# Ranks of single score tiles and weight chunks, and inverse sums loaded in two halves, in a fused attention and two-MLP kernel

## The chip, the cores and the metric

The kernel runs on one core of one Trainium2 chip. The metric is the device time in microseconds (us) of one execution; less is better. The engines are named as in the profile: PE (TensorE), PEld (its weight loads), DVE (VectorE), ACT (ScalarE), POOL (GpSimd) and SP (SyncE, which issues nearly all DMAs).

## The reference

Three layers follow each other, all in float32.

```python
scores = scale * q @ k.T                      # 4 batches, 8 heads, 576 x 576, head size 64
scores = where(scores >= max(scores) - tau, scores, -1e6 * 1000)
attn = exp(scores - max(scores))
attn = attn / (sum(attn) + 1e-9)
x = (attn @ v)                                # to 2304 tokens x 512
h = x @ w_in                                  # 512 x 2048
y = (h * sigmoid(h)) @ w_out                  # 2048 x 512
out = ((y @ w_a) * (y @ w_b)) @ w_o2          # 512 x 1536, 1536 x 512
```

## The kernel before, in words

**Stages.** Attention works on pairs of heads (16 pairs over 4 batches); each pair has a block of 4 score tiles (queries 0 to 255) and one of 5 tiles (queries 256 to 575), 144 tiles of 128 x 576 in all. In the first batch all the blocks of 4 come first, then the blocks of 5. A tile goes through these steps in `softmax` (L506): `scores` on PE into a PSUM bank (L530, from tile 54 on L523); `lowest` on DVE, which scales and finds the minimum (L539); `threshold` on DVE (L547, L545 in the first 16 tiles); `exp` on ACT (L553, L551 in the first 16); `mask` on DVE, which zeroes what lies under the threshold and sums the rest (L556). The first 16 tiles take turns in two banks, `sa` and `sb`; from then on `sa` alone is used and is free again after `lowest`. `weigh` (L575) transposes the masked tile on PE (`turn`, L589), copies it out on ACT (L597, L599), and multiplies by v (`values`, L638).

**The sums.** The masked weights are not divided; the product is. DVE inverts the sums (L488), PE transposes them beside the product (L643), ACT copies both to SBUF (`evacuate`, L659). A small DMA stores the inverse sums to DRAM (`store_sums`, L663), a second one loads them back, spread over 64 partitions for each of the two heads (`load_sums`, L670), POOL multiplies (`divide`, L673) and a third DMA stores x, transposed, to DRAM (`store`, L677). There is one buffer for x and one for the loaded sums. From tile 54 on, each head's q and k (one buffer, `qk0`) are split into two parts by ACT (L448), DVE (L451) and POOL (L454) ahead of the scores.

**The first MLP** reads x back by blocks of 256 tokens (later 512) (`load_x`, L727) and runs unit by unit: `mlp1_up` (L766), tanh and gate (L776 to L785), `mlp1_down` (L826). It fills PE beside attention and goes on alone once attention has ended. Its weights come in 32 chunks of 512 KB; `split_weight` (L326) loads one (L345) and takes it apart: ACT (L349, L354), DVE (L360, `join` L365), a sum on POOL or DVE (L370), the high part on ACT (L374), the low part on DVE (L378). A unit needs its chunks.

**The second MLP** (L1133, L1219) streams prepared weights and has no part in the change.

**The order** is worked out in Python while the kernel is built, by the class `Plan`. Each step is a task with an engine, a cost, a rank and the tasks it waits for. `run` plays the tasks through by their costs; an engine that comes free takes the ready task of the lowest rank:

```python
                if kind == "ready":
                    heapq.heappush(ready[x["engine"]], (x["rank"], x["n"]))
```

The order so found is then written out, and on the chip every engine runs its list strictly in that order. Score tile n has rank n (its mask n - 1, its transposes n + `R_T`, its q/k load n + `R_LD`); first-MLP units have ranks from `R_MLP` = 1000 up and so give way to attention; weight chunk i has rank `W_AT + W_STEP * i`, 2 + 1.3 i. DMAs are tasks of SP with a landing time of their cost, size and a `slack`. Where the plan shows idle time of PE ahead of a transpose, `turn` puts dummy transposes in front of it (L586), one for each 109 ns of 60% of that gap, at most 16.

## Time and profile before

| | us |
|---|---|
| median of 3 runs (lowest, highest) | 1130.11 (1128.37, 1130.49) |
| the profiled execution, its own time | 1129.17 |
| span of the profile | 1127.4 |
| PE busy (share of the span) | 1097.6 (97%) |
| DVE busy | 830.4 (74%) |
| ACT busy | 571.5 (51%) |
| POOL busy | 163.9 (15%) |

The span runs from the first to the last instruction of the program; the time of an execution holds a little around it. Busy shares are means over stages with different limits: attention with the first MLP beside it lasts until about 505 us, the rest of the first MLP until about 729 us, the second MLP to the end. The granted clock of PE was 0.996 of full speed over the span. Which engine paces a stage is read from the windows and waits of that stage.

### The profile page before, as it was taken

Reading aid. Unit: us, or ns where it says so; the run is one execution under the profiler, and the core shown is the slowest. Engines: PE = TensorE matmul, PEld = TensorE weight load, DVE = VectorE, ACT = ScalarE, POOL = GpSimd, SP = SyncE. Lnnn points to the kernel's source line nnn. Section 1 sums busy time; section 2 is a strip of 40 time slices with the busy share of each in tenths; the row PEclk is TensorE's granted clock in tenths of the full one; section 3 lists DMA queues with packets and bytes.
Section 4 is the critical chain, followed back from the end, with each engine's and each line's share of the span. In section 5 each row is a group of like instructions: output and inputs, shape, how many; then the busy total and the mean of one; then the engine's idle time right before and its main releaser. Section 6 shows DMA issues by size and latency. Waiting matters only on the chain.

```text
span 1127.4 us, 19460 instructions
## 1 busy us (share of the span) xinstructions
PE 1097.6 (97%) x7104; PEld 980.1 (87%) x7104; DVE 830.4 (74%) x1722; ACT 571.5 (51%) x1012; POOL 163.9 (15%) x308
## 2 busy tenths in 40 slices
PE   8879989999999999999999999999999999999998
PEld 6557767988899888899988888899999999999998
DVE  7878988888888898866898884256884668536664
ACT  6877776777677776765666552211242114401132
POOL 2452101323433433213000000000000000000000
PEclk9999999999999999999999999999999999999999
DMA  5564552544544343326898844488889888888882
GB/s 181 188 191 136 178 176 76 162 123 131 164 133 138 128 152 124 91 69 203 281 312 275 275 154 162 152 253 257 250 309 304 256 254 253 277 285 251 251 253 80
DMA packets 114975, 222.27 MB, mean 197 GB/s; under 512 B 8112, under 2 KB 75328, under 8 KB 114880
## 3 DMA queue, kind: packets, MB, share of 16 engines
q1 hardware_dynamic: 114736, 221.03, 61.9%
q8 instruction: 56, 0.92, 0.3%
q14 instruction: 39, 0.32, 0.1%
q10 hardware_dynamic: 144, 0.00, 0.0%
HBM read 173.74 MB, written 47.26 MB: 196 GB/s over the span
## 4 chain that ended last, share of the span: by engine, by line
PE 58%; DMA 1%; issue 1%; POOL 0%; DVE 0%; ACT 0%; SPq 0%; DVEq 0%; ACTq 0%
PE pr L1133 23%; PE pr L1219 11%; PE hb L766 6%; PE hc L766 5%; PE sb L826 3%; PE yc L826 2%; PE yd L826 2%; PE ye L826 2%; PE yf L826 2%; PE av L638 1%; PE tp L589 1%; DMA yr<-yT_d 1%; PE sa L523 1%; DMA qk<-qk 0%; POOL sp L454 0%
## 5 line engine op out<-in xcount | busy, mean ns | idle before, releaser
L1133 PE MATMUL pr<-w 128*128 128x384 f32 x1512 | 262.6, 334 | 0.0
L1133 PEld LDWEIGHTS pr<-w 128*128 128x128 f32 x1512 | 262.2, 188 | 0.1
L766 PE MATMUL hb<-xh,w 128*128 128x256 f32 (+1 forms) x704 | 157.5, 314 | 5.6 <-DVE th L779 4.6
L766 PEld LDWEIGHTS hb<-xh,w 128*128 128x128 f32 x704 | 114.3, 192 | 17.5 <-DVE th L779 5.8
L1219 PE MATMUL pr<-zh,w 128*128 128x384 f32 x504 | 128.4, 336 | 0.0
L556 DVE SCALAR_TENSOR_TENSOR e<-t,thr,e 128x576 f32<-128x576 f32 x128 | 109.7, 857 | 18.0 <-ACT e L553 16.6
L539 DVE TENSOR_SCALAR_CACHE_REDUCE t<-sa,nscale 128x576 f32<-128x576 f32 x128 | 103.8, 811 | 20.0 <-PE sa L523 16.3
L589 PE MATMUL tp<-ident,e 128*128 128x128 f32 (+1 forms) x706 | 106.1, 279 | 9.5 <-DVE e L556 6.6
L553 ACT ACTIVATE e<-t,min 128x576 f32<-128x576 f32 x128 | 99.3, 776 | 27.5 <-DVE t L539 27.2
L766 PE MATMUL hb<-xl,w 128*128 128x256 f32 (+1 forms) x352 | 107.7, 306 | 0.0
L589 PEld LDWEIGHTS tp<-ident,e 128*128 128x128 f32 (+1 forms) x706 | 76.6, 135 | 32.2 <-issue 15.1
L826 PE MATMUL sb<-gh,w 128*128 128x256 f32 (+1 forms) x576 | 95.9, 299 | 0.0
L1219 PEld LDWEIGHTS pr<-zh,w 128*128 128x128 f32 x504 | 91.1, 188 | 0.0
L826 PEld LDWEIGHTS sb<-gh,w 128*128 128x128 f32 x576 | 79.7, 190 | 7.2 <-issue 2.5
L1219 PE MATMUL pr<-zl,w 128*128 128x384 f32 x252 | 84.8, 336 | 0.1
L454 POOL TENSOR_TENSOR sp<-qk,sp 64x115 fp32r<-64x115 f32 (+1 forms) x100 | 61.7, 648 | 70.7 <-ACT sp L448 42.0
L1145 ACT COPY yo<-pr 128x384 f32<-128x384 f32 x18 | 8.6, 480 | 123.7 <-PE pr L1133 123.7
L523 PE MATMUL sa<-sp 128*128 128x288 f32 (+1 forms) x400 | 70.3, 301 | 0.0
L766 PEld LDWEIGHTS hb<-xl,w 128*128 128x128 f32 x352 | 67.5, 192 | 3.1 <-POOL xl L735 0.2
L984 ACT CAST zh<-z 128x768 fp32r<-128x768 f32 x45 | 37.6, 836 | 61.5 <-PE pr L1219 39.1
L673 POOL TENSOR_TENSOR x<-x,xi 128x128 f32<-128x128 f32 (+2 forms) x80 | 40.1, 525 | 195.1 <-DMA xi<-r_d 99.2
L779 DVE SCALAR_TENSOR_TENSOR th<-th,hb 128x256 f32<-128x256 f32 (+1 forms) x88 | 41.0, 466 | 37.2 <-ACT th L776 36.5
(159 smaller groups left out, 2011.9 us busy)
## 6 DMA issues: line engine op xcount, KB each, us to landing
w<-wab_d SPq DMA_DIRECT2D x126, 512.0 KB
w<-wo_d SPq DMA_DIRECT2D x63, 512.0 KB
qk<-qk SPq DMA_DIRECT2D x20, 576.0 KB
wab_d<-aw SPq DMA_DIRECT2D x11, 896.0 KB
wab_d<-uw SPq DMA_DIRECT2D x11, 896.0 KB
wraw<-w_in SPq DMA_DIRECT2D x16, 512.0 KB
wraw<-w_out SPq DMA_DIRECT2D x16, 512.0 KB
wo_d<-uw SPq DMA_DIRECT2D x9, 896.0 KB
```

Source lines behind the costliest of these rows:

```text
L454: nc.gpsimd.tensor_tensor(out=s["t"][D:, 0, o], in0=s["r"][D:, o], in1=s["t"][D:, 0, o].bitcast(F32), op=ALU.subtract)
L523: nc.tensor.matmul(s["s"][:r + m, j, :NH], lhsT=hd["t"][:, 0, c - r:c + m], rhs=hd["t"][:, k, j * NH:(j + 1) * NH], start=(k == 1), stop=( ...
L539: nc.vector.tensor_scalar(out=s["t"], in0=s["s"][:, :, :NH], scalar1=nscale, scalar2=None, op0=ALU.mult, op1=ALU.min, accum_out=s["min"])
L553: nc.scalar.activation(out=s["e"], in_=s["t"], func=AF.Exp, scale=-1.0, bias=s["min"])
L556: nc.vector.scalar_tensor_tensor(out=s["e"], in0=s["s"][:, :, :NH] if early else s["t"], scalar=s["thr"], in1=s["e"], op0=ALU.is_ge if ear ...
L589: nc.tensor.transpose(t["tp"][:m, j * P:(j + 1) * P], e["e"][:, o:o + m], ident)
L673: nc.gpsimd.tensor_tensor(out=s["x"][:, o], in0=s["x"][:, o], in1=s["i"][:, o], op=ALU.mult)
L766: nc.tensor.matmul(s["h"], lhsT=w[:, a, o:o + P], rhs=xx, start=(c == 0 and k == 0), stop=(c == NC - 1 and k == 2))
L779: nc.vector.scalar_tensor_tensor(out=s["t"], in0=s["t"], scalar=1.0, in1=s["h"], op0=ALU.add, op1=ALU.mult)
L826: nc.tensor.matmul(ys[j][e // per][:, e % per * tn:(e % per + 1) * tn], lhsT=w[:, a, e * P:(e + 1) * P], rhs=gs[j, f][g], start=(f == 0 an ...
L1133: nc.tensor.matmul(bank[:, m, :TN], lhsT=w["w"][:, 2 * m + k, a], rhs=y[i][x][:, k, :TN], start=(i in (1, 6, 5) and k == 0 and q == 0), st ...
L1219: nc.tensor.matmul(bank[:, c, :TN], lhsT=w["w"][:, 2 * e + c, a], rhs=z[x][:, e], start=(i in (1, 6, 5) and sl == 0 and e == 0 and q == 0) ...
```

## The change

Four things are edited. Line numbers of the kernel after are higher by 5 to 12 (L539 becomes L548, L556 becomes L565, L547 becomes L556, L670 becomes L682, L677 becomes L689).

First, 26 score tiles get a rank of their own: `at(n)` adds a number from a table to n, and the ranks of that tile's scores, minimum, threshold, exponential, mask and transposes go by it, as do the loads of q, k and v that start at that tile and the inversion and product of the block that ends there. Second, 14 of the 32 weight chunks get such an addition (`W_SHIFT`), from -13.8 to +4.5. Third, the load of the inverse sums is issued as two DMAs, one for each head's 64 partitions. Fourth, the planner counts two issues for that load and half the slack (1000 in place of 2000 ns).

```diff
+SHIFT = {1: 0.3, 2: 2.6, 5: -0.5, 7: -0.6, 8: 1.2, 10: -0.4, 11: -2.0, 14: -0.3, 19: -2.2, 20:
...
+W_SHIFT = {2: 0.3, 6: -0.1, 7: -4.1, 9: 0.4, 13: 3.6, 14: 0.3, 15: -3.8, 18: -2.3, 21: -2.8, 26:
...
-        ld = dma(n + R_LD, P * 4 * (cols.stop - cols.start), load, take=[raw])
+        ld = dma(at(n) + R_LD, P * 4 * (cols.stop - cols.start), load, take=[raw])
...
+    def at(n):
+        return n + SHIFT.get(n, 0)
...
+        n = at(n)
         cost = 4 * pe_ns(NH) * len(parts) if parts[0][0]["split"] else 850
...
+            r = at(r)
...
-            r = r_d[b, c, 4 * half * P:4 * half * P + 2 * nq].rearrange("(k o t) -> k o t", k=2, o=1)
-            nc.sync.dma_start(out=s["i"][:, :nq], in_=r.broadcast_to((2, D, nq)))
+            for k in range(2):
+                r = r_d[b, c, 4 * half * P + k * nq:4 * half * P + (k + 1) * nq].rearrange("(o t) -> o t", o=1)
+                nc.sync.dma_start(out=s["i"][k * D:(k + 1) * D, :nq], in_=r.broadcast_to((D, nq)))
...
-        ld = dma(-1, P * 4 * nq, load_sums, after=[st], take=["xi"], slack=SLACK)
+        ld = dma(-1, P * 4 * nq, load_sums, n=2, after=[st], take=["xi"], slack=SLACK // 2)
...
-    w1 = [t for i in range(32) for t in w1_chunk(i, W_AT + W_STEP * i)]
+    w1 = [t for i in range(32) for t in w1_chunk(i, W_AT + W_STEP * i + W_SHIFT.get(i, 0))]
```

What the new ranks do is seen in the order of the instructions. DVE, tiles 18 and 19 of the kernel before: minimum (L539), threshold (L547) and mask (L556), with steps of a weight chunk (L365, L378) between.

```order
L539 TENSOR_SCALAR t,min<-sa,nscale 128x576
L365 SCALAR_TENSOR_TENSOR wc<-wc,wraw 128x512
L547 TENSOR_SCALAR thr<-min,tadd 128x1
L556 SCALAR_TENSOR_TENSOR e,sum<-t,thr,e 128x576
L539 TENSOR_SCALAR t,min<-sa,nscale 128x576
L547 TENSOR_SCALAR thr<-min,tadd 128x1
L556 SCALAR_TENSOR_TENSOR e,sum<-t,thr,e 128x576
L378 TENSOR_TENSOR w<-wt,w 128x512
```

The same engine of the changed kernel, tiles 20 to 22 (L548 is the minimum, L556 the threshold, L565 the mask, L365, L370 and L383 the chunk):

```order
L383 TENSOR_TENSOR w<-wt,w 128x512
L365 TENSOR_SCALAR wraw<-wraw 128x512
L548 TENSOR_SCALAR t,min<-sa,nscale 128x576
L370 SCALAR_TENSOR_TENSOR wc<-wc,wraw 128x512
L565 SCALAR_TENSOR_TENSOR e,sum<-t,thr,e 128x576
L556 TENSOR_SCALAR thr<-min,tadd 128x1
L548 TENSOR_SCALAR t,min<-sa,nscale 128x576
L565 SCALAR_TENSOR_TENSOR e,sum<-t,thr,e 128x576
```

Before, a tile's mask follows its own minimum and threshold. Now, behind the minimum of tile 21, come a chunk step, the mask of tile 20, the threshold of 21 and the minimum of 22, and only then the mask of 21.

PE of the kernel before, the first first-MLP matmuls (L766) beside scores (L530), dummy transposes (L586) and transposes (L589):

```order
L766 MATMUL hb<-xh,w 128x256 x2
L766 MATMUL hb<-xl,w 128x256
L586 MATMUL tp<-ident 128x128 x6
L589 MATMUL tp<-ident,e 128x128 x4
L530 MATMUL sa<-qk_600 128x288 x2
L586 MATMUL tp<-ident 128x128 x6
L589 MATMUL tp<-ident,e 128x128 x4
```

The same place of the changed kernel (L778 for L766, L539 for L530, L596 for L586, L599 for L589):

```order
L778 MATMUL hb<-xh,w 128x256 x2
L778 MATMUL hb<-xl,w 128x256
L539 MATMUL sa<-qk_616 128x288 x2
L596 MATMUL tp<-ident 128x128 x2
L599 MATMUL tp<-ident,e 128x128 x4
L599 MATMUL tp<-ident,e 64x128 x2
```

The scores have moved ahead of the transposes, and 2 dummy transposes stand where there were 6. Over the whole program 98 dummy transposes become 66.

SP of the kernel before, around one load of inverse sums in the third stage of attention (L663 stores the sums, L670 loads them, L444 loads q and k, L677 stores x):

```order
L471 DMA v<-v 128x640
L663 DMA r_d<-x 5x128
L670 DMA xi<-r_d 128x1x320
L444 DMA qk_2901<-qk 128x1152
L926 DMA wab_d<-aw 128x7x256
L677 DMA xT_d<-x 128x320
```

The same place of the changed kernel:

```order
L674 DMA r_d<-x 5x128
L477 DMA v<-v 128x640
L682 DMA xi<-r_d 64x320 x2
L449 DMA qk_2830<-qk 128x1152
L938 DMA wab_d<-aw 128x7x256
L689 DMA xT_d<-x 128x320
```

One load of 128 partitions has become two of 64; what follows it in the queue is the same.

## Rows read from the trace of the kernel before

**Rows 1.** the page, its first line

```profile
span 1127.4 us, 19460 instructions
```

**Rows 2.** busy us by stretch: length, PE, PEld, DVE, ACT, POOL, clock, DMA share, GB/s

```profile
51.00:109.00 58.00, 52.04 (x363) 36.16 (x364) 46.48 (x121) 43.14 (x84) 25.27 (x53) 0.97 0.52 161
109.00:198.00 89.00, 82.67 (x610) 62.33 (x608) 80.07 (x203) 66.73 (x133) 10.68 (x19) 0.98 0.47 145
198.00:505.00 307.00, 301.86 (x2443) 269.86 (x2440) 256.46 (x694) 217.05 (x419) 101.56 (x174) 1.00 0.41 129
505.00:1127.00 622.00, 617.86 (x3413) 583.17 (x3412) 406.35 (x588) 205.44 (x310) 8.88 (x19) 1.00 0.76 242
```

**Rows 3.** waits of DVE, 51 to 109 us: total us, times, longest

```profile
DVE e L556 <- ACT e L553: 6.8, 10, 1.5
DVE w L378 <- ACT w L374: 2.5, 2, 1.7
```

**Rows 4.** waits of DVE, 109 to 198 us

```profile
DVE e L556 <- ACT e L553: 1.4, 3, 0.6
```

**Rows 5.** timeline, DVE, one tile: start us, us, what, [idle before, releaser]

```profile
57.72 0.82 DVE L539 TENSOR_SCALAR_CACHE_REDUCE t<-sa,nscale 128x576 f32<-128x576 f32 x1 [0.92 <-PE sa L530]
58.59 0.21 DVE L547 TENSOR_SCALAR thr<-min,tadd 128x1 f32<-128x1 f32 x1
59.81 0.82 DVE L556 SCALAR_TENSOR_TENSOR e<-t,thr,e 128x576 f32<-128x576 f32 x1 [1.01 <-ACT e L553]
```

**Rows 6.** DVE by line, 0 to 197.7 us: count | busy us, mean ns | idle before

```profile
L556 DVE SCALAR_TENSOR_TENSOR e<-t,thr,e 128x576 f32<-128x576 f32 x36 | 30.4, 845 | 8.7 <-ACT e L553 8.3
L378 DVE TENSOR_TENSOR w<-wt,w 128x512 fp32r<-128x512 f32 x32 | 22.2, 692 | 2.8 <-ACT w L374 2.5
L785 DVE TENSOR_TENSOR gl<-th,gh 128x256 fp32r<-128x256 f32 x17 | 7.6, 446 | 0.5 <-ACT gh L782 0.3
L779 DVE SCALAR_TENSOR_TENSOR th<-th,hb 128x256 f32<-128x256 f32 x17 | 7.1, 417 | 4.2 <-ACT th L776 4.1
L848 DVE TENSOR_SCALAR yo<-sb 128x512 f32<-128x512 f32 x1 | 0.7, 691 | 0.8 <-ACT yo L846 0.8
```

**Rows 7.** all engines by line, 0 to 200 us: the dummy transposes

```profile
L586 PE MATMUL tp<-ident 128*128 128x128 f32 x98 | 14.5, 284 | 2.1 <-ACT pb L597 2.1
```

**Rows 8.** waits of PE, 198 to 505 us: total us, times, longest

```profile
PE hb L766 <- DVE th L779: 1.6, 2, 1.1
PE tp L589 <- ACT pb L597: 1.6, 3, 0.9
PE av L643 <- DVE sums L488: 1.0, 1, 1.0
```

**Rows 9.** timeline, ACT at two places

```profile
236.85 1.15 ACT L448 CAST sp<-qk 128x1152 fp32r<-128x1152 f32 x1 [1.60 <-DMA qk<-qk]
...
377.01 0.48 ACT L659 COPY x<-av 128x384 f32<-128x384 f32 x1 [3.90 <-DMA xT_d<-x]
```

**Rows 10.** chain of waits in order of time: start us, us, what

```profile
432.94 1.78 DMA xT_d<-x
...
460.39 4.23 issue
...
467.76 5.41 DMA qk<-qk
...
508.45 1.44 PE hb L766 x12
```

**Rows 11.** tile xi, who waited for it: us, times

```profile
  POOL sp L454: 22.3, 5
```

**Rows 12.** one us of that load's flight, columns as in rows 2

```profile
145.50:146.50 1.00, 1.00 (x9) 1.00 (x10) 1.00 (x4) 1.00 (x4) 0.00 (x0) 1.00 0.13 46
```

**Rows 13.** timeline, SP and POOL: one load of inverse sums and its division

```profile
142.29 0.50 SPq L670 DMA_DIRECT2D xi<-r_d  x1
...
149.05 1.00 POOL L673 TENSOR_TENSOR x<-x,xi 128x106 f32<-128x106 f32 x2 [22.21 <-ACT wc L354]
```

## The prediction, made before the changed kernel had run

> **What bounds the kernel now.** I read the windows first, to see which stretch has slack at all. The profiled span is 1127.4 us [rows 1]. From 505 us on TensorE (PE) has 617.9 busy of 622 us; from 198 to 505 it has 301.9 of 307, but from 51 to 198 only 52.0 of 58 and 82.7 of 89 [rows 2]. So after 198 us PE paces the kernel and its total work is fixed; what can be gained is idle PE time ahead of that, and a few gaps up to 505. Where PE has idle time, VectorE (DVE) is the busy one: 80.1 of 89 us from 109 to 198 [rows 2]. The lines of DVE up to 197.7 us name the point: 36 masks (L556) beside the 16 of the early tiles, thus tile 52, and all 32 low parts of weight chunks (L378) [rows 6]. After tile 52 no weight chunk loads DVE any more. I therefore work with two stretches: up to tile 52 DVE sets the time, after it PE does.

> Next the waits of DVE. From 51 to 109 us it waits 6.8 us in 10 pieces for the exponential of a score tile, and 2.5 us in two pieces for the rounded high part of a weight chunk [rows 3]; from 109 to 198 us the exponential costs another 1.4 us [rows 4]. The timeline shows the pattern: minimum of a tile until 58.54 (57.72 and 0.82 us), a 0.21 us threshold, then 1.01 us idle until the mask at 59.81 [rows 5]. Between the minimum and its mask DVE must have about 1.25 us of other work, or it stands.

> Last, the late transfers. PE's larger waits after 198 us are 1.6, 1.6 and 1.0 us in all, the longest 1.1, 0.9 and 1.0 [rows 8]. All three of those longest ones follow a late DMA: ACT stood 1.60 us for a q/k load just before 238 us and 3.90 us for the store that frees the x tile just before 377 [rows 9], and the chain of waits runs at 460 us from a 4.23 us stretch in which POOL stood, into a q/k load of 5.41 us, and on to PE [rows 10]. POOL stands there because the division of x waits for the inverse sums and the q corrections are queued behind it: 22.3 us in 5 such waits [rows 11]. One load of inverse sums, issued at 142.29, lets the division start at 149.05: 6.3 us after its 0.50 us issue [rows 13]. While little else flies, the DMA share is 0.13 [rows 12], that is 2.1 of 16 engines.

> **The change part by part.** Counted in the two instruction orders, up to the mask of tile 52 on DVE and its four transposes on PE:

> 1. *DVE work up to tile 52.* Same tiles, same 32 chunks; one first-MLP unit fewer (0.42 and 0.45 us) and one output halving fewer (0.69) [rows 6]: -1.5 us.

> 2. *Waits for the exponential.* Summing for each tile what the DVE work between minimum and mask lacks to 1.25 us: tiles 17 to 31, before 9.6 us over 12 short tiles, now 2.7 over 4, since another tile's mask, a threshold or a chunk step now stands in between. That is 72% less; of the measured 6.8 us [rows 3], -4.9. Tiles 32 to 52: 1.9 to nothing; of 1.4 measured [rows 4], -1.4. Tiles 1 to 16: 2.1 to 3.1; +1.0. Once, between tiles 24 and 25, two minima now follow each other with 0.2 us between, where the wait for a refilled score bank was 0.92 us [rows 5]: +0.7. The chunk whose low part came 1.8 us after its join, where the others have 2.6 to 2.9 and mostly do not wait, is spread out: of 2.5 us [rows 3], -2.0. Together -6.6 us. Ends: 0 if other waits fill the holes, -10.7 if all three rows go (6.8, 1.4, 2.5).

> 3. *First-MLP work left for later.* By tile 52 PE has done 18 up and 16 down matmuls fewer. At 1.44 us for 12 [rows 10] that is 4.1 us which must now be done after tile 52, where PE has no room: +4.1 us. This one has a single answer; later the deficit shrinks, but that only moves work inside the PE-paced stretch.

> 4. *Fillers.* The dummy transposes fall from 98 to 66. They lie in PE's idle time up to tile 52, covered by DVE's pace: 0. If PE were the pace there, 32 at 14.5 / 98 us [rows 7] would give -4.7.

> 5. *Two half loads of inverse sums.* Each adds one issue, 0.50 us [rows 13], 32 times, 16 us in all of the SP queue over some 490 us; what is queued behind is mostly the wait for that same load. So I cost the issues at nothing; uncovered, one issue is 0.5 us in front of a q/k load. For the load itself the nearest row on many engines is the store of the same x tile, 1.78 us to landing [rows 10]: a load of 1.78 and a second issue of 0.5 in place of 6.3 saves 4.0 us, at worst 0. I take the store's row, because the share of 0.13 says that two engines carry the load now, as many as its outermost dimension (the two halves) counts; a half has no such dimension and begins with its 64 rows. A load 4 us sooner covers the three waits of ACT and POOL (1.60, 3.90, 4.23), so the three long PE gaps go: 1.1 + 0.9 + 1.0, -3.0 us. Ends 0 and -4.2 (all of [rows 8]).

> [...]

> First-MLP input: the sums of the fourth pair come 3.3 us later in DVE work, its x 4.0 us sooner after them; I cost that at 0.

> Sum: -1.5 - 6.6 + 4.1 - 3.0 = -7.0 us. The profiled execution took 1129.17 us (span 1127.4 and 1.8 around it), so 1122.2 for one like it. The median of the runs, 1130.11, is 0.9 above it: **1123.1 us**.

> **The rivals.**

> *The holes fill again.* DVE and ACT wait for each other in turn, and the exponential's wait comes back as one for the score bank or the transposes. For it: DVE already waits for scores on other tiles, and two minima now meet. Against: the short tiles do fall from 12 to 4 in the very stretch with the waits. With part 2 at 0 and the rest as above, -0.4: 1129.7.

> *The halves are no faster,* so the change of the load does not do what it says: the two transfers follow each other on the same engines and the division still starts 6.3 us after the issue. The planner now allows such a load 1 us less, so it places its users no later. Against: the share of 0.13. Part 5 is 0, the rest holds: -4.0, 1126.1. [...]

> *Slower: PE runs dry of first-MLP work.* The weight chunks come 5 to 8 us of DVE work later between chunks 13 and 32, so the 34 matmuls are missing while PE stands, and are paid after tile 52. It decides where the DVE waits saved and the late transfers saved together stay under 0.3 us: with both at 0, -1.5 + 4.1 = +2.6, 1132.7; with the two losses of part 2 (1.0 and 0.7) on top, 1134.4. For it: the shift is certain, the saving is estimated. Against: 6.8 us of waits with a visible cause.

> **How the numbers follow.** A measurement of this kernel tells apart about 0.2%, 2.3 us. Forecast 0.60, holes filled 0.18, halves no faster 0.08, slower 0.14. The best bounds together, -1.5 - 10.7 + 4.1 - 4.2 = -12.3, give 1117.8, and some of the fillers' 4.7 us could add to it: low end 1115. The high end, 1131, takes in the first two rivals and leaves out the slower one. Faster by over 0.2% are nearly all of the forecast (0.57), the halves rival for the most part (0.06) and a little of the filled holes (0.04): 0.67. Slower: 0.14 and 0.02 of the filled holes: 0.16. The rest, 0.17, is no change.

> **What would show it.** Right: DVE's wait for the exponential between 51 and 109 us under 3 us; the mask of tile 52, at 197 us before, about 8 us sooner, near 189; the division some 2 to 3 us after the issue of the second half, and a high DMA share where 0.13 stood; no ACT wait over 1.5 us for a q/k load or an x store; PE full from tile 52 on. Wrong: tile 52 at 196 or later with new waits of DVE for scores; the division still 6 us behind; or new PE gaps between 198 and 505, since on tiles 101 to 144 the work between minimum and mask is scarcer than before (short by 11.4 us instead of 4.3), which I cost at 0 because PE paces that stretch.

## The result and the profile after

| | before | after |
|---|---|---|
| median of 4 runs each, us (lowest to highest) | 1129.61 (1128.37 to 1130.49) | 1113.49 (1112.92 to 1113.88) |
| span of the profiled execution, us | 1127.4 | 1112.0 |

After over before is 0.9858, with a 95% interval of 0.9841 to 0.9875: 16.1 us less, where 7.0 were forecast. The time lies under the low end of the range.

The page of the changed kernel, its first line and that of the engines:

```profile
span 1112.0 us, 19484 instructions
...
PE 1088.8 (98%) x7072; PEld 975.1 (88%) x7072; DVE 832.4 (75%) x1722; ACT 569.3 (51%) x1012; POOL 165.5 (15%) x308
```

Its windows, columns as in [rows 2]; the last two are the stretches that end with the mask of tile 52 and with that of the last tile, 144:

```profile
51.00:109.00 58.00, 53.46 (x390) 36.08 (x388) 52.68 (x139) 47.09 (x95) 28.41 (x52) 0.98 0.60 181
109.00:198.00 89.00, 85.43 (x643) 66.80 (x642) 85.19 (x213) 70.83 (x143) 18.13 (x30) 1.00 0.50 153
198.00:505.00 307.00, 306.11 (x2491) 276.53 (x2491) 251.50 (x677) 214.91 (x416) 95.88 (x175) 1.00 0.42 131
...
0.00:183.20 183.20, 166.38 (x1187) 118.50 (x1188) 167.03 (x437) 145.69 (x281) 56.60 (x114) 0.99 0.56 173
183.20:482.10 298.90, 297.74 (x2421) 267.93 (x2421) 257.08 (x694) 216.13 (x416) 98.03 (x173) 1.00 0.43 133
```

DVE is busy 52.68 of 58 us from 51 to 109 (46.48 before) and 85.19 of 89 from 109 to 198 (80.07). PE has 0.9 us without work from 198 to 505, where it had 5.1.

Its lines of DVE up to 183.3 us show how much sooner the same point comes. Here are all 36 masks and all 32 low parts that [rows 6] counted up to 197.7:

```profile
L565 DVE SCALAR_TENSOR_TENSOR e<-t,thr,e 128x576 f32<-128x576 f32 x36 | 30.3, 844 | 3.3 <-ACT e L562 3.3
L383 DVE TENSOR_TENSOR w<-wt,w 128x512 fp32r<-128x512 f32 x32 | 22.8, 712 | 1.8 <-ACT w L379 1.7
```

The wait of DVE for the exponential up to tile 52 is 3.3 us where it was 8.3, and tile 52 is 14.6 us sooner. The waits of DVE from 51 to 109 us answer to [rows 3]:

```profile
DVE e L565 <- ACT e L562: 3.3, 6, 1.1
DVE t L548 <- PE sa L539: 1.0, 2, 0.7
DVE w L383 <- ACT w L379: 0.5, 2, 0.4
```

Of PE's waits from 198 to 505 us [rows 8] one line is left:

```profile
PE hb L778 <- DVE th L791: 0.7, 1, 0.7
```

And one load of inverse sums, as [rows 13] has it, in the timelines of SP and POOL:

```profile
140.68 1.09 SPq L682 DMA_DIRECT2D xi<-r_d  x2
...
144.93 1.30 POOL L685 TENSOR_TENSOR x<-x,xi 128x128 f32<-128x128 f32 x2 [13.17 <-DMA xi<-r_d]
```

The division starts 3.2 us after the second issue, where 6.3 us stood after the only one. The DMA share of this flight says little of the halves, since a chunk load of 512 KB issued at 139.62 us is still under way beside them. Another pair, issued at 324.11 us, flies alone; its issues on SP and the window of one microsecond of its flight answer to [rows 12]:

```profile
324.11 1.12 SPq L682 DMA_DIRECT2D xi<-r_d  x2
...
325.50:326.50 1.00, 1.00 (x11) 1.00 (x10) 1.00 (x5) 0.97 (x3) 0.00 (x0) 1.00 0.56 127
```

The DMA share is 0.56 for the two halves together, that is 9.0 of 16 engines, where 0.13 stood for the whole load.

### The profile page after: what moved, and what is told of

It reads as the page before. It is cut to its first block, busy times and chain, and to the rows that moved or that the text cites. A ratio compares the mean times of both kernels' runs of the same rounds, so it can differ in the third digit from the quotient of the medians.

```text
span 1112.0 us, 19484 instructions
## 1 busy us (share of the span) xinstructions
PE 1088.8 (98%) x7072; PEld 975.1 (88%) x7072; DVE 832.4 (75%) x1722; ACT 569.3 (51%) x1012; POOL 165.5 (15%) x308
## 4 chain that ended last, share of the span: by engine, by line
PE 83%; DVE 6%; DMA 4%; ACT 3%; issue 2%; POOL 1%; SPq 0%; ACTq 0%; DVEq 0%; POOLq 0%
PE pr L1145 24%; PE pr L1231 12%; PE hb L778 11%; PE sb L838 8%; PE av L649 5%; PE hc L778 5%; PE tp L599 5%; PE sa L532 4%; PE yd L838 2%; PE yc L838 2%; PE yf L838 2%; PE ye L838 2%; DMA wraw<-w_in 2%; DMA qk<-qk 1%; DVE e L565 1%
## 5 line engine op out<-in xcount | busy, mean ns | idle before, releaser
L778 PE MATMUL hb<-xh,w 128*128 128x256 f32 (+1 forms) x704 | 156.0, 312 | 1.5 <-DVE th L791 1.0
L778 PEld LDWEIGHTS hb<-xh,w 128*128 128x128 f32 x704 | 113.3, 190 | 13.8 <-issue 4.3
L548 DVE TENSOR_SCALAR_CACHE_REDUCE t<-sa,nscale 128x576 f32<-128x576 f32 x128 | 103.7, 810 | 20.8 <-PE sa L532 19.2
L565 DVE SCALAR_TENSOR_TENSOR e<-t,thr,e 128x576 f32<-128x576 f32 x128 | 108.8, 850 | 13.1 <-ACT e L562 12.3
L599 PE MATMUL tp<-ident,e 128*128 128x128 f32 (+1 forms) x706 | 105.7, 278 | 6.2 <-DVE e L565 4.8
L778 PE MATMUL hb<-xl,w 128*128 128x256 f32 (+1 forms) x352 | 106.8, 303 | 0.0
L599 PEld LDWEIGHTS tp<-ident,e 128*128 128x128 f32 (+1 forms) x706 | 77.3, 135 | 27.5 <-issue 14.6
L778 PEld LDWEIGHTS hb<-xl,w 128*128 128x128 f32 x352 | 66.9, 190 | 2.8
L797 DVE TENSOR_TENSOR gl<-th,gh 128x256 fp32r<-128x256 f32 (+1 forms) x112 | 60.4, 539 | 9.0 <-ACT gh L794 8.9
```

The costliest lines, as they stand in the source:

```text
L548: nc.vector.tensor_scalar(out=s["t"], in0=s["s"][:, :, :NH], scalar1=nscale, scalar2=None, op0=ALU.mult, op1=ALU.min, accum_out=s["min"])
L565: nc.vector.scalar_tensor_tensor(out=s["e"], in0=s["s"][:, :, :NH] if early else s["t"], scalar=s["thr"], in1=s["e"], op0=ALU.is_ge if ear ...
L599: nc.tensor.transpose(t["tp"][:m, j * P:(j + 1) * P], e["e"][:, o:o + m], ident)
L778: nc.tensor.matmul(s["h"], lhsT=w[:, a, o:o + P], rhs=xx, start=(c == 0 and k == 0), stop=(c == NC - 1 and k == 2))
L797: nc.vector.tensor_sub(out=s["gl"], in0=s["t"], in1=s["gh"].bitcast(F32))
```

## The experiments

Each kernel was timed in five rounds beside the kernel before on the same chip; the ratios are to that. In brackets stand 95% intervals.

### The two parts of the change, apart

First, the kernel before with the halves alone; its planner counts one issue and the full slack, as it did:

```diff
-            r = r_d[b, c, 4 * half * P:4 * half * P + 2 * nq].rearrange("(k o t) -> k o t", k=2, o=1)
-            nc.sync.dma_start(out=s["i"][:, :nq], in_=r.broadcast_to((2, D, nq)))
+            for k in range(2):
+                r = r_d[b, c, 4 * half * P + k * nq:4 * half * P + (k + 1) * nq].rearrange("(o t) -> o t", o=1)
+                nc.sync.dma_start(out=s["i"][k * D:(k + 1) * D, :nq], in_=r.broadcast_to((D, nq)))
```

> The order of the kernel before, instruction for instruction, with the inverse sums loaded in two halves and nothing else changed. Theory (the new order gives about 11 of the 16 us, the halves the rest): the division starts 2 to 3 us after the second issue, ACT no longer waits for x stores and q/k loads after 198 us, and the time is 1124 to 1127 us. Rival, the halves serialize and are no faster: 1129.6 us. Rival, the halves are most of the gain, since a late transfer also holds up the tiles before 198 us: 1116 to 1120 us.

Measured: 1119.5 us, 0.9917 [0.9892, 0.9942]. Second, the changed kernel with these five lines the other way round: the new order, with the planner as it is in the changed kernel, and the load whole.

> The order of the changed kernel, instruction for instruction, with the inverse sums loaded whole, as before. Theory: 3 to 5 us slower than the changed kernel, 1116.5 to 1118.5 us, with ACT waits for the x store back after 198 us and the mask of tile 52 within 2 us of the changed kernel's 183.2. Rival, halves no faster: 1113.5. Rival, halves are most of the gain: 1124 us or more. If the two parts depend on each other, the loss here differs from the gain of the halves in the old order.

Measured: 1124.52 us, 0.9956 [0.9941, 0.9971]. The order is worth 4.7 us (4.0 forecast), the halves 9.8 us in the old order and some 11 in the new one (3.0 forecast). So one of the five terms is off.

Then the changed kernel without one of its two tables, first that of the chunks:

```diff
-    w1 = [t for i in range(32) for t in w1_chunk(i, W_AT + W_STEP * i + W_SHIFT.get(i, 0))]
+    w1 = [t for i in range(32) for t in w1_chunk(i, W_AT + W_STEP * i)]
```

> The changed kernel with the additions to the ranks of the weight chunks left out. Theory (the tile ranks fill the waits for the exponential, the chunk ranks only spread the chunk steps): 2 to 5 us slower than the changed kernel, 1115.5 to 1118.5 us, mask of tile 52 at 184 to 188. Rival, the chunk ranks carry the gain, since later chunks are what lets tiles and first-MLP input run ahead: 1121 us or more, mask of tile 52 at 192 or later.

Measured: 1113.35 us, 0.9857 [0.9835, 0.988], the time of the whole change. No gain of the chunk table can be told. Now that of the tiles:

```diff
-        return n + SHIFT.get(n, 0)
+        return n
```

> The changed kernel with the additions to the ranks of the score tiles left out. Theory: most of the waits of DVE for the exponential between tiles 17 and 31 come back (5 us or more in 51 to 109 us, 3.3 in the changed kernel), mask of tile 52 at 190 or later, 1119 to 1123 us. Rival, the chunk ranks carry the gain: 1114 to 1117 us.

Measured: 1119.42 us, 0.991 [0.9888, 0.9932], the time of the halves alone. The ranks of the tiles carry the order's part. Two signs that this expectation named did not come, though: DVE waits 3.7 us for the exponential from 51 to 109 us, not 5 or more, and tile 52 ends at 188.3 us, not at 190 or later. Its wait for a refilled score bank is 2.9 us there; the changed kernel has 3.3 and 1.0 us. That the tile ranks bring the gain is shown; that they bring it through the wait for the exponential alone is not.

### Where the halves gain

Quarters in place of halves, with two issues more for each load:

```diff
-            for k in range(2):
-                r = r_d[b, c, 4 * half * P + k * nq:4 * half * P + (k + 1) * nq].rearrange("(o t) -> o t", o=1)
-                nc.sync.dma_start(out=s["i"][k * D:(k + 1) * D, :nq], in_=r.broadcast_to((D, nq)))
+            for k in range(4):
+                r = r_d[b, c, 4 * half * P + k // 2 * nq:4 * half * P + (k // 2 + 1) * nq].rearrange("(o t) -> o t", o=1)
+                nc.sync.dma_start(out=s["i"][k * 32:(k + 1) * 32, :nq], in_=r.broadcast_to((32, nq)))
```

> The changed kernel with the inverse sums loaded in four quarters of 32 partitions: two more issues for each load on the SP queue, no less data. Theory (an issue in front of the wait for the division costs nothing, and the quarters land no later than the halves): 1112.5 to 1115 us. Rival, SP issue time is on the path, some 0.5 us twice for each of 32 loads: 1118 us or more.

Measured: 1114.69 us, 0.987 [0.9852, 0.9889]. The 64 further issues cost little or nothing, as part 5 had it for its own. Halves only up to tile 54, 12 of the 32 loads, the others whole:

```diff
+            if b > 1 or (b == 1 and c > 1):
+                r = r_d[b, c, 4 * half * P:4 * half * P + 2 * nq].rearrange("(k o t) -> k o t", k=2, o=1)
+                nc.sync.dma_start(out=s["i"][:, :nq], in_=r.broadcast_to((2, D, nq)))
+                return
```

> New order, instruction for instruction; halves for the 12 blocks up to tile 54, whole loads for the 20 after. By tile times the halves saved 5.8 us up to tile 52 and 5.2 after it. Theory, both stretches gain by themselves: 1117.5 to 1120 us. Rival, all comes from the stretch after tile 52, as the prediction had it: 1123 us or more. Rival, what is saved early carries through to the end and the late loads are hidden: 1113 to 1115.

Measured: 1117.78 us, 0.9895 [0.9877, 0.9914]. Against the whole load in this order the first 12 halves give 6.7 us, against all halves the last 20 give 4.3. Both stretches gain, also the one for which part 5 had counted nothing; which of the two shares is the larger, the intervals leave open. Next, the load whole with a planner that is told of it:

```diff
-        ld = dma(-1, P * 4 * nq, load_sums, n=2, after=[st], take=["xi"], slack=SLACK // 2)
+        ld = dma(-1, P * 4 * nq, load_sums, after=[st], take=["xi"], slack=3700)
```

> New ranks, whole load, but the planner is told how long that load really takes (slack 3700 ns and one issue, some 6 us from issue to division). If the slow load costs time only because the order was made for a faster one: 1114 to 1118 us, with SP waiting less for POOL. If the latency itself is what costs, in whatever order: 1121 us or more.

Measured: 1136.86 us, 1.007 [1.0055, 1.0086]. A planner that knows the latency does not make it harmless. This kernel has another order as well, so it says no more than that.

### One instruction list, two loads

The new order with the whole load and the changed kernel issue the same instructions in the same order on every engine but for SP's second issue of each such load. So the start of an instruction in the one can be subtracted from its start in the other, and every step in that lag is a place where the slower load cost time. Timeline of ACT, whole load, at four of the steps:

```profile
31.02 0.62 ACT L379 CAST w<-wt 128x512 fp32r<-128x512 f32 x1 [1.57 <-POOL wt L375]
...
59.78 0.62 ACT L379 CAST w<-wt 128x512 fp32r<-128x512 f32 x1 [2.46 <-POOL wt L375]
...
126.65 0.67 ACT L354 ACTIVATE wt<-wraw 128x512 uint32<-128x512 uint32 x1 [2.73 <-DMA wraw<-w_out]
...
259.84 1.15 ACT L453 CAST sp<-qk 128x1152 fp32r<-128x1152 f32 x1 [2.12 <-DMA qk<-qk]
```

The same four instructions in the changed kernel:

```profile
29.57 0.62 ACT L379 CAST w<-wt 128x512 fp32r<-128x512 f32 x1 [0.25 <-POOL wt L375]
...
57.15 0.62 ACT L379 CAST w<-wt 128x512 fp32r<-128x512 f32 x1 [0.47 <-POOL wt L375]
...
120.65 0.69 ACT L354 ACTIVATE wt<-wraw 128x512 uint32<-128x512 uint32 x1 [1.43 <-DMA wraw<-w_out]
...
251.57 1.16 ACT L453 CAST sp<-qk 128x1152 fp32r<-128x1152 f32 x1 [0.49 <-DMA qk<-qk]
```

The whole load is behind by 1.5, 2.6, 6.0 and 8.3 us. Three different ways lead there.

*POOL's queue.* Timeline of POOL ahead of the first step, whole load:

```profile
29.29 0.87 POOL L684 TENSOR_TENSOR x<-x,xi 128x128 f32<-128x128 f32 x2 [1.63 <-DMA xi<-r_d]
30.12 0.86 POOL L375 TENSOR_TENSOR wt<-wc,wt 128x128 uint32<-128x128 uint32 x2
```

and in the changed kernel:

```profile
27.84 0.87 POOL L685 TENSOR_TENSOR x<-x,xi 128x128 f32<-128x128 f32 x2 [0.30 <-DMA xi<-r_d]
28.66 0.87 POOL L375 TENSOR_TENSOR wt<-wc,wt 128x128 uint32<-128x128 uint32 x2
```

The sum of a weight chunk is queued behind the division, ACT waits for the sum and DVE for ACT. DVE's waits up to tile 52 for the high part of a chunk, whole load first, changed kernel second:

```profile
DVE w L383 <- ACT w L379: 5.9, 8, 1.5
```

```profile
DVE w L383 <- ACT w L379: 1.7, 4, 0.8
```

*SP's queue.* The chunk that ACT takes at 126.65 had been issued at 122.99, behind the load of a first-MLP input that waited for an x store, behind that store, which waited for the division at 117.22. In the changed kernel these are 116.81 and 110.17. Waits of SP up to 505 us, whole load first, changed kernel second:

```profile
SPq L688 <- POOL x L684: 131.0, 30, 9.0
```

```profile
SPq L689 <- POOL x L685: 72.8, 26, 5.6
```

*The transfers behind the load.* Timeline of SP ahead of the fourth step, whole load:

```profile
252.05 0.55 SPq L681 DMA_DIRECT2D xi<-r_d  x1
252.97 0.34 SPq L449 DMA_DIRECT2D qk<-qk  x1
```

and in the changed kernel:

```profile
245.45 1.12 SPq L682 DMA_DIRECT2D xi<-r_d  x2
246.67 0.54 SPq L449 DMA_DIRECT2D qk<-qk  x1
```

The load of q and k was issued 0.4 us behind the issue of the whole load and 0.1 us behind those of the halves, and ACT got it 6.5 us after the issue behind the whole load and 4.4 us behind the halves.

### Taking the ways apart

Seven kernels with the whole load try to free the x buffer, SP's queue or POOL's queue, singly and together, or to bring the sums to the load sooner; the third way above, the transfers behind the load, is left as it is in all of them. The x buffer, which ACT must wait to refill, is freed early when the product goes into the buffer of the inverse sums:

```diff
-            nc.gpsimd.tensor_tensor(out=s["x"][:, o], in0=s["x"][:, o], in1=s["i"][:, o], op=ALU.mult)
+            nc.gpsimd.tensor_tensor(out=s["i"][:, o], in0=s["x"][:, o], in1=s["i"][:, o], op=ALU.mult)
...
-            nc.sync.dma_start(out=xT_d[c, :, t0:t0 + nq], in_=s["x"][:, :nq])
+            nc.sync.dma_start(out=xT_d[c, :, t0:t0 + nq], in_=s["i"][:, :nq])
```

> New order, whole load; the division writes into the buffer of the loaded sums and the store reads it, so the one x buffer comes free before the store instead of after its landing. ACT waited 2.9 us for that store with this order and the whole load (1124.5 us). If the x buffer is how a slow load costs time: 1119 to 1122 us. If it is the queues of SP and POOL: 1123.5 to 1125.

Measured: 1123.45 us, 0.9951 [0.9934, 0.9968], no difference from the 1124.52 that can be told. Then the small store of the sums, issued by ACT in `evacuate`, behind the copy, in place of `store_sums`:

```diff
+            nc.scalar.dma_start(out=r_d[b, c, k0 * P:(k0 + len(tiles)) * P].rearrange("(k p) -> k p", p=P),
+                                in_=s["x"][:len(tiles), nq:nq + P])
```

> New order, inverse sums loaded whole (1124.5 us as it stood), but the small store of the inverse sums ahead of that load is issued by ACT, right behind the copy that fills it, and not by SP. The load itself takes as long as before. If what counts is the time from the sums to x (the chain theory), the chain is shortened at its other end, by whatever SP's queue held the store back: 1118 to 1122. If what counts is what stands behind the x store in SP's queue (the queue theory), little changes, since the division still comes 6 us after the load's issue: 1123.5 to 1125. ACT pays 32 issues of some 0.5 us, at most +2 where ACT is waited for.

Measured: 1129.88 us, 1.0006 [0.999, 1.0023]; neither theory. Its premise was false: in the kernel it started from, SP issues that store 0.03 us after the copy (median of 32), so there was nothing to shorten. Where its loss of 5.4 us against 1124.52 comes from stays open. Then the x store, put behind whatever load SP issues next:

```diff
-            nc.sync.dma_start(out=xT_d[c, :, t0:t0 + nq], in_=s["x"][:, :nq])
+            flush()
+            pending.append(lambda: nc.sync.dma_start(out=xT_d[c, :, t0:t0 + nq], in_=s["x"][:, :nq]))
```

> New order, inverse sums loaded whole (1124.5 us as it stood), but SP issues each x store only behind the next load (of q and k, of a weight chunk, of a first-MLP input or of inverse sums), so that this load no longer stands behind a store that waits for the division. The load of the inverse sums is as slow as before. Queue theory: most of the 11 us that the halves gave in this order comes back, 1115 to 1119, and SP's wait for x, 131 us in 30 pieces up to 505 us, falls under 80. Chain theory: 1123.5 to 1126, a little worse where the late store holds back the x buffer or the first MLP's input.

Measured: 1162.2 us, 1.0286 [1.0256, 1.0315]. SP's wait for x fell to 40.2 us, below the 80 that the queue theory wanted, and the kernel lost 38 us; waits of ACT up to 505 us:

```profile
ACT x L683 <- DMA xT_d<-x: 38.0, 12, 5.7
```

The next load is often itself one that waits, and the one x buffer then stays occupied. Both edits on the changed kernel did the same:

> The changed kernel (1113.5 us) with both edits: the sums stored by ACT and each x store issued behind the next load. If the queue or the chain still costs time at 4 us per load, as 72.8 us of SP's waits for x and 11.5 us of ACT's waits for loads suggest, it gains part of what is left: 1109 to 1112. If PE is full enough by now (291.1 of 292 us from 198 to 490 us, 85.4 of 89 before), 1113 to 1114.5.

Measured: 1163.72 us, 1.0298 [1.0267, 1.0328]. So the store was put back only where a load of q and k or of a chunk follows it directly in SP's queue (any other DMA of SP issues a pending store first):

```diff
             nc.sync.dma_start(out=s["r"], in_=qk2[b, h])
+            flush()
...
-            nc.sync.dma_start(out=xT_d[c, :, t0:t0 + nq], in_=s["x"][:, :nq])
+            late.append(lambda: nc.sync.dma_start(out=xT_d[c, :, t0:t0 + nq], in_=s["x"][:, :nq]))
```

> New order, inverse sums loaded whole (1124.5 us as it stood). SP issues an x store behind a load of q and k or of a weight chunk only where that load is the next thing in its queue, some 10 of 32 places; there the load no longer waits for the division. If the loads behind the store carry a good part of the 11 us that the halves gave in this order: 1118 to 1122, with ACT's waits for q/k and chunk loads, 17.5 us before, down to some 10. If SP's queue is not the path, or the late store costs as much at the x buffer: 1124 to 1127.

Measured: 1140.84 us, 1.0084 [1.006, 1.0108]; the wait for the x buffer is still 22.3 us in 7 pieces. The same with the x buffer freed early:

> As the kernel before this one, and x is written into the buffer of the inverse sums, so that ACT can fill the x buffer again without waiting for the store (1123.5 us for this alone). If SP's queue is the path and only the x buffer stood against it: 1115 to 1119. If what counts is POOL's queue, where chunk sums and q corrections stand behind the division: 1122.5 to 1125, as neither edit brings the division sooner.

Measured: 1123.12 us, 0.9929 [0.991, 0.9949]. The 17.7 us between these two show what the single x buffer costs once a store is late. Against 1123.45 without the moved stores there is no difference to be told. Then POOL's queue, in the kernel with the x buffer free: the three chunk sums for which ACT had waited 1.96, 2.03 and 1.39 us are made by DVE.

```diff
+            if key in (('in', 3, 0), ('in', 0, 1), ('out', 4)):
+                if o.start:
+                    return
+                eng, o = nc.vector, slice(0, 512)
```

> New order, whole load, x written into the buffer of the inverse sums (1123.5 us, tile 31 at 97.8 and tile 52 at 189.8), and three of the 32 chunk sums, the ones for which ACT waited 1.96, 2.03 and 1.39 us since they stood behind a division on POOL, are made by DVE instead. If POOL's queue is a path by which the late load costs time up to tile 52: the 5.4 us go, less 3 x 0.7 of DVE, tile 31 near 95, tile 52 at 186.5 to 187.5, 1120 to 1121.5 us. If not, DVE's work is added: tile 52 at 190 or later, 1123.5 to 1126.

Measured: 1123.06 us, 0.994 [0.9917, 0.9962], again none. The three waits are gone, and at 60 us ACT is 3.4 us ahead of the kernel it started from; at 90 us it is 0.2 us behind it. All three edits together:

> The same three sums by DVE, x written into the buffer of the inverse sums, and an x store issued behind a q/k or chunk load that directly follows it (1123.1 us without the sums, tile 52 at 188.9). If the x buffer, SP's queue and POOL's queue are the three paths and add up: 1118 to 1121, tile 52 near 186. If they stand in for one another, or POOL's q corrections after tile 52 carry the rest: 1121 to 1124.

Measured: 1121.29 us, 0.9928 [0.9905, 0.9951]. Tile 52 ends at 186.3 us, between the 189.1 of the whole load and the 183.2 of the halves. From there to tile 144 it takes 302.6 us, where the whole load took 304.0 and the halves 298.9; that is one execution of each, and not enough to call it a gain. None of these edits, alone or together, returned more than some 3 of the 11 us. That with one way free the next one sets the time would explain it, but is argued and not shown.

### A version of the changed kernel, and the dummy transposes

Two edits were also put on the changed kernel, first the x store behind a load that follows it directly:

> The changed kernel (1113.5 us) with each x store behind a q/k or chunk load that follows it directly. Where the store waits for the division less than the load behind it can spare, nothing: 1113 to 1115. If SP's queue still costs: 1110 to 1112. If the late store comes to hold the x buffer: 1115 to 1118.

Measured: 1128.2 us, 0.9982 [0.9965, 0.9999], 15 us lost. Then the product into the buffer of the inverse sums (the diff of the x buffer above):

> The changed kernel (1113.5 us), with x written into the buffer of the inverse sums, so that ACT never waits for the x store (1.7 us of such waits are left in it up to 505 us). 1112 to 1114: the wait is short already, and the same edit gave 1 us with whole loads.

Measured: 1111.47 us, 0.9828 [0.9806, 0.9851]. It is the shortest time of all; its interval overlaps with the changed kernel's, so that it beats the kernel before is shown, and that it beats the changed one is not.

Part 4 was tried on the kernel before, with no dummy transposes (they are no part of the result):

```diff
-                for _ in range(min(16, int(FILL * t["task"]["gap"] / 109))):
+                for _ in range(0):
```

> The kernel before without its 98 dummy transposes (14.5 us of PE, no part of the result), everything else as it was. Forecast's part 4 (they lie in PE's idle time, DVE sets the pace there): 1129.6 within 2, with the granted clock between 51 and 198 us not lower than 0.97. If they stood on PE's path: up to 14.5 us less, by the part that 32 of them were bounded at some 4.7 less for a third, so 1115 to 1125. If they keep the clock up: the clock of these stretches falls and the time rises by 2 or more.

Measured: 1136.22 us, 1.0062 [1.004, 1.0085]. Two of its windows:

```profile
10.00:20.00 10.00, 8.33 (x35) 4.59 (x37) 7.71 (x21) 7.44 (x14) 2.71 (x7) 0.67 0.26 80
51.00:109.00 58.00, 47.46 (x298) 31.04 (x297) 45.10 (x116) 41.60 (x81) 23.81 (x51) 0.85 0.52 154
```

The granted clock is a mean of 0.67 and 0.85 here, where the kernel before had 1.00 and 0.97. Tile 52 comes at 202.5 in place of 197.8.

## Why the prediction was wrong

**Parts 1 to 3 held in their sum.** They forecast tile 52 to come 1.5 + 6.6 = 8.1 us sooner; in the new order with the whole load it comes 8.7 us sooner (189.1 for 197.8). Part 3 wanted 4.1 us back after it. From tile 52 to tile 144 that kernel takes 304.0 us for 301.2, and behind it 0.9 us more: 3.7. The whole order gave 4.7 us where -1.5 - 6.6 + 4.1 make 4.0. DVE's work up to tile 52 is 166.0 us for 167.5, the 1.5 of part 1, and its waits together are 21.7 us for 27.9, 6.2 less where part 2 forecast 6.6. By its rows, part 2 met this with luck. Waits of DVE up to tile 52, the new order with the whole load:

```profile
DVE w L383 <- ACT w L379: 5.9, 8, 1.5
DVE e L565 <- ACT e L562: 4.1, 5, 1.5
...
DVE th L790 <- ACT th L787: 0.2, 1, 0.2
```

The wait for the exponential of tiles 17 to 52 fell by 4.2 us (8.3 to 4.1), where 6.3 were forecast. The wait for the chunk's high part, which was to lose 2.0 of 2.5, rose to 5.9. The wait for tanh, which part 2 left out, fell from 4.1 to 0.2 and made up for it. That the holes fill again has fallen as a rival: DVE's wait for the exponential between 51 and 109 us is 1.5 us with the order alone and 3.3 in the changed kernel, in place of 6.8. That PE runs dry has fallen too.

**Part 4 held in its number, not in its reason.** 98 dummy transposes became 66, the granted clock from 51 to 198 us was 0.98 and 1.00 (0.97 and 0.98 before), and the order's sum left no room for more. But they are not free to leave out: the run without any took 1136.22 us, 1.0062 of the kernel before, with a granted clock of 0.85 from 51 to 109 us.

**Part 5 is the term that was mis-sized: -3.0, with an end at -4.2, where 9.8 us and some 11 were measured.** It even took the halves for faster than they are. It took 4.0 us off each load; by the loads for which POOL stood waiting, the time from the first issue's start to the division fell from a median of 5.7 us to 3.5 in the old order and from 6.0 to 4.3 in the new one, some 2 us. (The one load of [rows 13], from which it worked, took 6.8 by this measure.) The step that failed came after it: "A load 4 us sooner covers the three waits of ACT and POOL (1.60, 3.90, 4.23), so the three long PE gaps go: 1.1 + 0.9 + 1.0". This looked for the load's price only where PE paces the kernel and only in PE's waits.

Up to tile 52 it counted nothing, and there the halves gave 3.9 us in the old order (193.9 for 197.8) and 5.9 in the new (183.2 for 189.1). There DVE sets the time, and a late load reaches it through ACT: the wait for the chunk's high part in the new order (5.9 us to 1.7), and in the old one the waits for tanh, which the prediction's own [rows 6] showed with 4.1 us and did not follow. With the halves in the old order, waits of DVE up to tile 52:

```profile
DVE th L780 <- ACT th L777: 0.8, 3, 0.4
```

After tile 52 the term was too small as well: 4.8 us in the old order and 5.1 in the new. The windows up to tile 52 and from there to tile 144, first of the kernel before, then of its order with the halves:

```profile
0.00:197.80 197.80, 177.65 (x1252) 126.96 (x1254) 167.49 (x440) 148.81 (x285) 53.43 (x115) 0.98 0.52 161
197.80:499.00 301.20, 296.06 (x2398) 265.61 (x2399) 255.11 (x691) 214.68 (x414) 100.69 (x172) 1.00 0.42 131
...
0.00:193.90 193.90, 176.28 (x1252) 126.42 (x1254) 168.14 (x440) 148.74 (x284) 55.81 (x115) 0.98 0.53 164
193.90:490.30 296.40, 294.74 (x2398) 265.28 (x2399) 255.52 (x693) 215.04 (x414) 104.21 (x172) 1.00 0.43 134
```

The same of the new order with the whole load:

```profile
0.00:189.10 189.10, 167.90 (x1185) 118.24 (x1185) 166.00 (x437) 145.78 (x281) 57.11 (x114) 0.99 0.54 167
189.10:493.10 304.00, 299.82 (x2423) 268.48 (x2422) 255.87 (x694) 216.65 (x416) 97.12 (x173) 1.00 0.43 131
```

Beside the last two windows of the changed kernel these are the same instructions (437 of DVE up to tile 52). In the second stretch PE has 4.2 us without work here and 1.2 with the halves, which is the 3.0 forecast. The other 2.1 us are in PE's busy time. Two matmuls more fall into the stretch (2423 for 2421), by estimate 0.6 us, from the 291 ns that an L778 matmul takes there in the changed kernel; what the rest is, no run here shows.

Of the signs that the prediction named, the wait for the exponential is 3.3 us (under 3), the division comes 3.2 us behind the second issue (2 to 3), and ACT's longest waits for a q/k load and an x store are 1.5 and 1.7 us (none over 1.5): all nearly so, none quite. PE full from tile 52 on did come, with 297.7 of 298.9 us. Tile 52 was named for 189, where the order alone put it; the halves took it to 183.

**The rival "The halves are no faster"** has fallen: the division comes some 2 us sooner. The whole load ran at a share of 0.13, two halves at 0.56. Part 5 read the 0.13 as two engines and tied them to the two halves in the load's outermost dimension; the runs show the share with each form of the load, not what sets it. The third way above is a q/k load that lands late behind the whole one. The packets in the traces show it: 4.5 us after the start of their issue, the six q/k loads counted below behind the whole load had started 50, 94, 112, 113, 114 and 124 of their 128 rows, and the four behind the halves all 128. The load of the fourth step is the one with 50. What held the missing rows back is not shown; on which engine a packet ran, the traces do not show.

**What stays open.** The x buffer, SP's queue and three chunk sums of POOL's queue were freed in several combinations. Together they returned some 3 of the 11 us; by the interval that is not certain. How much of the rest is q/k loads behind the whole load, the third way, and how much q corrections behind the division on POOL, was not tried; the view that the prediction used for the latter [rows 11] does not measure it, since in the changed kernel, with the faster load, it shows more:

```profile
  POOL sp L459: 36.8, 8
```

## What to carry to other kernels

Price a late transfer by everything that stands in order behind its user, on each queue, and not by the waits of the engine that paces one stage. To find where it costs, keep the instruction order, change the transfer alone, and subtract the start times of the same instructions. Taking one wait out of several can show little, as the single edits did here. And a buffer with a single copy must be freed before its store is moved: the same move cost 16 us with the x buffer bound and nothing with it freed.
